# Values of the last batch's closing in seven products, gated products on GpSimd

## The chip, the cores and the metric

The kernel runs on one core of one Trainium2 chip. The core has five engines that run side by side, each through its own queue in order: TensorE (PE; its weight loads are shown apart as PEld), VectorE (DVE), ScalarE (ACT), GpSimd (POOL) and SyncE (SP, which issues most of the DMAs). Matrix products land in PSUM, of which the kernel uses eight banks of 512 f32 numbers per partition; everything else is in SBUF. The metric is the time of one execution on the device in microseconds, and the figure for a kernel is the median of several runs.

## The reference

Two layers follow each other. The first is attention in which a query sees only the keys of its own cluster, the second a gated feed-forward layer:

```python
mask = q_assign[:, :, :, None] == k_assign[:, :, None, :]
scores = np.where(mask, scale * q @ k.T, -1e9)
attn = softmax(scores) @ v                       # 4 batches, 8 heads, 768 x 64
x = attn.transpose(0, 2, 1, 3).reshape(3072, 512)
gate = 1.0 / (1.0 + np.exp(-(x @ w_gate)))       # 512 x 1536
val = x @ w_val                                  # 512 x 1536
out = (gate * val) @ w_out                       # 1536 x 512
```

Inputs and output are f32; the kernel multiplies in f16 and adds in f32.

## The kernel before

The program is written out step by step, in an order that is set by hand: a table of numbers (`SCHED`) gives each piece of preparation a step at which it is issued, and each engine runs its instructions in the order of issue. There are 384 attention steps, 96 per batch. A step is one score product (`sc`, L1026), its exponential on ACT (`es`, L1031) and, a few steps later, three products with the values (`av`, L1049). Between them the feed-forward layer of the batch before is fed in: groups of four matmuls for a gate (`g`, L531, tanh on ACT at L537) and for a value (`v`, L547), joined on DVE into `hT` (L552).

Scores, gates, values and logits (`lg`, L435) share a ring of four PSUM banks; two further pairs of banks are named `o` and `av`. A bank is taken again when the last operation that reads its old content is done.

The attention output is kept as x/2, so that the gate is tanh(x/2) + 1 = 2 sigmoid(x), and times (x/2) w_val that is gate times value.

The last batch has no attention behind it that could hide its feed-forward layer. It runs in `closing`. The hidden units come in 12 column blocks of 128, the 768 tokens in two halves of 384. Two column blocks (`FC0`) are done plainly, four matmuls for each block and half. The other ten form five column pairs, and the gates of a pair (two blocks by two halves) come as a 2 x 2 block product in seven products in place of eight (Strassen-Winograd). Each of the seven is two matmuls of 384 columns. They need four differences of the weights (`T` 1 to 4, made by `fin_weights`, one DVE operation for each, L602; eight in all for the two halves of `wg`) and four of the tokens (`S`, by `fin_tokens`, L616).

The class `Unit` holds a pair. Its products p1, p6, p7 and p4 add up in one PSUM bank `x`, and after each of them the bank's content is one step of the result: ACT copies it out (`c1`, `c12`, `c22`, and for p4 the last gate itself). p5 and p3 add up in a second bank `y`, p2 has a third; DVE adds these to the copies (`plus`, L650), and ACT takes the tanh. The values of a pair are computed in the plain way, one group of four matmuls for each block and half, in the period of the next pair (`Unit.v`, `hidden`). So a period of `closing` has 14 matmuls for the gates of one pair and 16 for the values of the pair before: 30.

What follows is the product with `w_out`, also in seven products, over three pairs of token blocks (`m0`, `ma`, `mb`); it needs sums of `hT` that DVE makes (`Sums.make`, called as `part`), and ends with the stores. The scratch tiles of `closing` are taken from the pool of the transposed heads, `T`; in the trace all of them bear that name.

Of the kernel before, what the change touches and what calls it, by code (L numbers as in the profile page):

```python
# [99 lines left out]
def kernel(  # L100
# [18 lines left out]
    NCH = S // 128  # L119
# [466 lines left out]
    def fin_weights(i, t):  # L586

        fin_room()
        a = FC0 // 2 if i == 0 else 0
        q = lambda k, j: wg[i][:, 2 * k : 2 * k + 2].rearrange(  # L590
            "p d (q j) f -> p d q j f", j=2
        )[:, :, a:, j]
        tw = lambda t: fin["kq"[i], (t - 1) // 2][:, (t - 1) % 2].rearrange(
            "p (d q f) -> p d q f", d=2, q=3
        )
        fin["T", i, t] = tw(t)
# [5 lines left out]
        DVE.tensor_tensor(cut(z), cut(x), cut(y), ALU.subtract)  # L602
# [25 lines left out]
    def fin_plain(xT, fc, blk):  # L628
        b, st = B - 1, []

        def gate():
            if fc == 0:
                need(*(("x", b, p, 3 * blk + c) for p in range(NP) for c in range(3)))
                HB[b, blk] = htp.tile([128, NFC, 384], HP, name="hT")
            g = fin_group(xT, 0, fc, blk)
            st.append(thp.tile([128, 384], FP, name="th"))
            ACT.activation(st[0], g, AF.Tanh)

        return [(NDC * 163, gate), (NDC * 163, lambda: hidden(xT, fc, blk, st[0]))]

    def hidden(xT, fc, blk, th):
        w = fin_group(xT, 1, fc, blk)
        DVE.scalar_tensor_tensor(HB[B - 1, blk][:, fc], th, 1.0, w, ALU.add, ALU.mult)  # L643

    def closing(xT):
# [5 lines left out]
        fin_tokens(xT, 4)  # L651
        room = [tp.tile([128, 12, 128], HP, tag="T", name="T") for _ in range(7)]
        slot = []
        for t in room[:4]:
# [4 lines left out]
        for m, n in ((m0, 0), (ma, 0), (mb, 1)):  # L659
            for i in (1, 2, 3):  # L660
                if n == 0:
                    m.of[i] = sump.tile([128, HF, 128], HP, tag="sum", name="sum")
                else:
                    m.of[i] = room[4 + i // 2][:, HF * (i % 2) : HF * (i % 2) + HF]
        m0.of[4], ma.of[4], mb.of[4] = room[4][:, 0:HF], room[6][:, 0:HF], room[6][:, HF:12]

        class Unit:
            def __init__(u, n, f):
                u.f, u.i, u.q = f, f // WQ, f % WQ // 2
                n = n % 2  # L670
                u.c1, u.c12, u.c22, u.c21 = slot[4 * n : 4 * n + 4]

            def mm(u, o, k, start, stop):
                T_ = lambda t, d: fin["T", u.i, t][:, d, u.q, :]
                W_ = lambda k_, j, d: wg[u.i][:, 2 * k_ + d, (u.f + j) % WQ, :]
# [13 lines left out]

            def p1(u):  # L690
                u.x = out_bank()[:, 0:384]
                u.mm(u.x, 1, True, True)
                ACT.activation(u.c1, u.x, AF.Copy)

            def p5(u):
                u.y = avp.tile([128, 512], FP, tag="av", name="av")[:, 0:384]
                u.mm(u.y, 5, True, True)

            def p6(u):
                u.mm(u.x, 6, False, True)  # L700
                ACT.activation(u.c12, u.x, AF.Copy)

            def p2(u):
                z = bank(512, name="gz")[:, 0:384]
                u.mm(z, 2, True, True)
                plus(u.c1, z, u.c1)

            def p7(u):
                u.mm(u.x, 7, False, True)
                ACT.activation(u.c22, u.x, AF.Copy)  # L710
                ACT.activation(u.c1, u.c1, AF.Tanh)

            def sum22(u):
                plus(u.c22, u.y, u.c22)

            def p4(u):
                u.mm(u.x, 4, False, True)
                ACT.activation(u.c21, u.x, AF.Tanh)
                ACT.activation(u.c22, u.c22, AF.Tanh)

            def p3(u):
                u.mm(u.y, 3, False, True)
                plus(u.c12, u.y, u.c12)

            def tanh12(u):
                ACT.activation(u.c12, u.c12, AF.Tanh)
# [5 lines left out]
        seq = []  # L732
        units = [Unit(n, f) for n, f in enumerate((6, 2, 8, 4, 10))]
        old = [f for fc in range(FC0) for _, f in fin_plain(xT, fc, 1)]
        def part(i, m, c0, c1, eng=None):
            return lambda: m.make(i, c0, c1, eng)

        extra = {
            3: [part(3, m0, 0, 4), part(3, ma, 0, 4)],
            4: [part(1, m0, 0, 4), part(2, m0, 0, 4)],  # L740
        }
        for n, u in enumerate(units):
            w = old if n == 0 else [lambda i=i, u=units[n - 1]: u.v(i) for i in range(4)]
            l = units[n - 1] if n else None
            ex = list(extra.get(n, []))
            e = lambda k: [ex.pop(0) for _ in range(min(k, len(ex)))]
            seq += [u.p1, w[0]] + ([l.p3] if l else []) + e(1) + [u.p5, u.p6]
            seq += ([l.tanh12] if l else []) + [w[1], u.p2, u.p7, w[2], u.sum22]
            seq += [w[3]] + e(1) + [u.p4]
# [54 lines left out]
        u = units[-1]  # L804
        both = lambda m, *c: [part(1, m, *c), part(2, m, *c)]
        seq += [lambda: u.v(0), part(1, ma, 0, 4), u.p3, u.tanh12, p0(1), lambda: u.v(1), part(2, ma, 0, 4), pa(1)]
        seq += [lambda: u.v(2), *both(m0, 4, HF), pb(1), lambda: u.v(3), l0([(0, HD)]), *both(ma, 4, HF)]
        seq += [la([(0, HD)]), part(1, mb, 0, HF), p0(6), part(2, mb, 0, HF), p0(5)]
        seq += [part(3, m0, 4, HF), part(3, ma, 4, HF), pa(6), part(4, m0, 0, HF), pa(5), part(3, mb, 0, HF)]
        seq += [p0(7), part(4, ma, 0, HF), pb(6), part(4, mb, 0, HF), pb(5)]  # L810
        seq += [pa(7), p0(4), p0(3), pb(7), pa(4), pa(3), pb(4), pb(3), lb([(0, HD // 2), (HD // 2, HD)])]
# [273 lines left out]
    def at(i, f):  # L1085
        bg.setdefault(max(i, step_no[0] - 0.5), []).append(f)
# [575 lines left out]
    for b in range(B):  # L1662
        xT = xtp.tile([128, NDC, S], HP, tag="xTb", name="xTb")
        key = min(b, 1)
        for i in range(2 if b else NPT):
            u = BASE[b] + (DONE0[i] if b == 0 else 96 - 12 * halved(b) if i == 0 else 96)
            lag = SCHED.get(f"lag{key}{i}", 8)
            if b == B - 1:
                if i == 0:
                    at(u + lag, lambda xT=xT: queue.extend(a for fc in range(FC0) for a in fin_plain(xT, fc, 0)))  # L1670
                    at(u + SCHED.get("fs1", 9), lambda xT=xT: (fin_tokens(xT, 1), fin_tokens(xT, 2)))
                    at(BASE[b] + 48 + SCHED.get("fs3", 17), lambda xT=xT: fin_tokens(xT, 3))
                    for k, s_ in enumerate(SCHED["fw"]):
                        at(s_, lambda k=k: fin_weights(1 - k // 4, 1 + k % 4))
# [56 lines left out]
```

## Time and profile before

| | |
|---|---|
| median of 3 runs | 321.93 us (321.38 to 322.49) |
| profiled execution | 320.28 us |
| its span, first to last instruction | 318.5 us |
| granted TensorE clock | 1.00 |
| attention steps, first score to last | about 9 to 269 us |
| `closing` with the plain column blocks | from 271.6 us |
| five pairs' periods | 274.2 to 299.3 us |
| output product | to 315.1 us (last matmul) |

The profile is one execution. Times in its rows are microseconds from the span's start. In a row of the timeline stand start, duration, engine, line, operation, and output from input, with the number of instructions that were merged, and in brackets the idle time of the engine before it with what ended it. A group of matmuls is drawn to the end of its last result, which overlaps the start of the next group. In a row of groups stand the busy time, the mean duration of one in ns, and the idle time before them.

### The profile page before, as it was taken

To read this page: it belongs to the slowest core of one execution; us is meant where nothing else is said; L and a number is where in the kernel's file an instruction comes from. 1 tells how busy PE (TensorE), PEld (TensorE's weight loads), DVE (VectorE), ACT (ScalarE), POOL (GpSimd) and SP (SyncE) were. 2 spreads that over 40 slices of the span, in tenths; PEclk is the share of its full clock that TensorE was granted. 3 is DMA by queue.
4 is the path that set the end of the run, shared out by engine and by line. 5 is a ranking of instruction groups with operands and counts; after the bars stand their busy time and mean duration, and the time that the engine had idled before them with its cause. 6 is when DMAs were issued, how large, how long until landed. Compare 5 with 4: busy or idle time off the path is not lost.

```text
span 318.5 us, 9195 instructions
## 1 busy us (share of the span) xinstructions
PE 312.2 (98%) x3500; PEld 221.1 (69%) x3500; DVE 233.7 (73%) x615; ACT 240.4 (75%) x545; POOL 109.0 (34%) x145
## 2 busy tenths in 40 slices
PE   7999999999999999999999999999999999999995
PEld 5888666766766666666777678666777678666685
DVE  6899656778687777686779678776766777668873
ACT  6688998797889887877767786887878886466521
POOL 5888454244434275423233342523202111000000
PEclk9999999999999999999999999999999999999999
DMA  7999998748859988977775555872612120300014
GB/s 197 374 266 187 262 158 132 180 95 244 243 102 178 188 231 133 204 211 149 110 204 139 180 111 147 255 106 52 112 24 67 42 27 20 138 3 0 1 35 165
DMA packets 77996, 45.16 MB, mean 142 GB/s; under 512 B 56896, under 2 KB 75520, under 8 KB 77952
## 3 DMA queue, kind: packets, MB, share of 16 engines
q1 hardware_dynamic: 73840, 39.66, 51.3%
q0 software_dynamic: 3680, 4.72, 8.9%
q8 instruction: 27, 0.44, 0.6%
q10 hardware_dynamic: 432, 0.20, 0.2%
q14 instruction: 17, 0.14, 0.2%
HBM read 28.34 MB, written 6.29 MB: 109 GB/s over the span
## 4 chain that ended last, share of the span: by engine, by line
PE 95%; DVE 2%; POOL 1%; issue 0%; ACT 0%; POOLq 0%; DVEq 0%
PE sc L1026 19%; PE g L531 15%; PE v L547 15%; PE av L1049 11%; PE o L954 9%; PE v L622 5%; PE o L825 5%; PE lg L435 2%; PE o L685 2%; PE o_end L763 2%; PE lg L422 1%; PE o L763 1%; PE av L763 1%; PE av L685 1%; PE t_ps L1275 1%; PE oh_ps L1335 1%
## 5 line engine op out<-in xcount | busy, mean ns | idle before, releaser
L1031 ACT ACTIVATE es<-sc 128x384 f16<-128x384 f32 x384 | 174.1, 492 | 38.6 <-PE sc L1026 29.9
L1026 PE MATMUL sc<-T 128*128 128x384 f16 x384 | 117.5, 326 | 0.4 <-DVE T L1356 0.4
L1049 PEld LDWEIGHTS <-es 128*128 128x128 f16 x1152 | 81.3, 98 | 35.1 <-ACT es L1031 0.2
L1049 PE MATMUL av<-va,es 128*128 128x65 f16 x1152 | 97.6, 194 | 0.0
L552 DVE SCALAR_TENSOR_TENSOR hT<-th,v 128x384 f16<-128x384 f32 x72 | 39.8, 553 | 38.3 <-PE av L1049 34.1
L531 PE MATMUL g<-xTb,wg 128*128 128x384 f16 x288 | 58.5, 326 | 0.2 <-DVE hT L552 0.2
L547 PE MATMUL v<-xTb,wv 128*128 128x384 f16 x288 | 58.6, 326 | 0.1
L376 POOL TENSOR_TENSOR xp<-t,rec 128x384 f16<-128x384 f32 (+1 forms) x30 | 21.6, 721 | 96.9 <-DVE rec L373 48.1
L537 ACT ACTIVATE th<-g 128x384 f32<-128x384 f32 x72 | 35.4, 491 | 8.7 <-PE g L531 6.7
L531 PEld LDWEIGHTS <-wg 128*128 128x128 f16 x288 | 27.9, 97 | 14.3 <-issue 0.4
L547 PEld LDWEIGHTS <-wv 128*128 128x128 f16 x288 | 28.0, 98 | 13.9 <-issue 0.3
L1026 PEld LDWEIGHTS <-T 128*128 128x128 f16 x384 | 37.1, 97 | 0.7 <-DVE T L1356 0.7
L1592 POOL TENSOR_TENSOR hl<-kraw,hl 128x384 f16<-128x384 f32 x22 | 20.2, 920 | 41.4 <-DVE hl L1591 24.3
L1592 POOL TENSOR_TENSOR hl<-qraw,hl 128x384 f16<-128x384 f32 x22 | 21.2, 962 | 11.1 <-DVE hl L1591 11.1
L825 PE MATMUL o<-wo,hT 128*128 128x512 f16 x72 | 19.9, 379 | 0.0
L371 DVE TENSOR_TENSOR t<-av,sv 128x390 f32<-128x390 f32 (+1 forms) x30 | 14.4, 480 | 7.2 <-PE av L1049 5.2
L622 PE MATMUL v<-xTb,wv 128*128 128x384 f16 x96 | 18.9, 326 | 0.0
L901 DVE TENSOR_TENSOR ob<-o,ob 128x256 f32<-128x256 f32 (+1 forms) x28 | 15.0, 549 | 4.7 <-PE o L954 3.2
L954 PE MATMUL o<-wo,hT 128*128 128x256 f16 x108 | 16.8, 273 | 0.0
L954 PEld LDWEIGHTS <-sum 128*128 128x128 f16 x144 | 14.0, 97 | 3.3
L643 DVE SCALAR_TENSOR_TENSOR hT<-T,v 128x384 f16<-128x384 f32 x20 | 11.0, 552 | 5.3 <-PE v L622 5.3
L450 DVE TENSOR_REDUCE lgs<-lg 128x192 f32<-128x384 f32 x23 | 12.7, 551 | 2.3 <-PE lg L435 2.3
(207 smaller groups left out, 445.2 us busy)
## 6 DMA issues: line engine op xcount, KB each, us to landing
vraw<-in_v_dram SPq DMA_DIRECT2D x15, 384.0 KB, 5.0
kraw<-in_k_dram SPq DMA_DIRECT2D x14, 384.0 KB, 4.9
qraw<-in_q_dram SPq DMA_DIRECT2D x12, 384.0 KB, 4.1
out_dram<-ob SPq DMA_DIRECT2D x17, 256.0 KB, 2.2
wg<-in_moe_w_gate_dram POOLq DMA_DIRECT2D x2, 768.0 KB, 9.6
wv<-in_moe_w_val_dram POOLq DMA_DIRECT2D x2, 768.0 KB, 10.5
wo<-in_moe_w_out_dram POOLq DMA_DIRECT2D x2, 768.0 KB, 9.4
T<-ohT SPq DMA_DIRECT2D x44, 24.0 KB, 1.9
```

Source lines behind the costliest of these rows:

```text
L376: (eng or POOL).tensor_tensor(x, t[:, 0:nq, 0:64], bcast(rec[:, 0:nq], 64), ALU.mult)
L531: PE.matmul(out=g[:, 0:n], lhsT=wg[fc // WQ][:, dc, fc % WQ, :], rhs=xT[:, dc, t0 : t0 + n], start=(dc == 0), stop=(dc == NDC - 1),)
L537: ACT.activation(th[:, 0:n], g[:, 0:n], AF.Tanh)
L547: PE.matmul(out=w[:, 0:n], lhsT=wv[fc // WQ][:, dc, fc % WQ, :], rhs=xT[:, dc, t0 : t0 + n], start=(dc == 0), stop=(dc == NDC - 1),)
L552: DVE.scalar_tensor_tensor(HB[b, blk][:, fc, 0:n], st[0][:, 0:n], 1.0, w[:, 0:n], ALU.add, ALU.mult)
L622: PE.matmul(out=o[:, 0:384], lhsT=w[:, dc, fc % WQ, :], rhs=xT[:, dc, 384 * blk : 384 * blk + 384], start=(dc == 0), stop=(dc == NDC - 1),)
L825: PE.matmul(out=o, lhsT=HB[b, blk][:, fc, bass.ts(t, 128)], rhs=wo[fc // WON][:, fc % WON, :], start=(fc == 0), stop=(fc == NFC - 1),)
L954: PE.matmul(out=st[z][:, e], lhsT=a[:, c, :], rhs=rhs[:, c, :], start=start and c + e == 0, stop=c == HF - 1, skip_group_check=True,)
L1026: PE.matmul(out=sc.rearrange("p (c t) -> p c t", t=128), lhsT=s["k"], rhs=s["q"], start=True, stop=True,)
L1031: ACT.activation(es, sc, AF.Exp, scale=SCALE)
L1049: PE.matmul(out=av[:, a0 + s["c0"] + i, :], lhsT=s["es"][:, bass.ts(i, 128)], rhs=VA[b, p][:, e, s["j"], :], start=(first and i == 0 and a ...
L1592: POOL.tensor_tensor(hl[:, :, 64:128], r, hl[:, :, 0:64], ALU.subtract)
```

## The change

The values of the first four pairs of `closing` are computed in seven products as well. The fifth pair keeps its four plain groups. What follows from it in the code:

- `fin_weights` makes four differences for each half of `wv` too, eight more DVE operations. Those of `wg` are issued at steps 327 to 344 in place of 354 to 371, and those of `wv` at the old steps. They are stored in the four `hl` tiles.
- `Unit` has a flag `w` (0 gate, 1 value). A value unit has its bank `x` from the `av` pair, `y` and the bank of p2 come from the ring. The values' p1 is taken out by DVE (`double`), the two other copies by ACT, with the factor 2 in them or in the sum (`twice`).
- The gate is now a sigmoid with scale 2, and the value carries the factor 2. This needs another function table on ACT; a small activation ahead of the first gate (`ACT.activation(r1, ones[:, 0:1], AF.Sigmoid)`) has it loaded.
- Three of the four gated products of a value unit (gate times value) go to POOL (`gated`); the fourth reads PSUM and stays on DVE (`out21`). The fifth pair's stay on DVE.
- A period is written anew: gate products of pair n, value products p1, p6, p5, p7, p2 of pair n-1, and its p4 and p3 in the period after. A full period has 28 matmuls.
- The pairs' order is 6, 2, 4, 8, 10 in place of 6, 2, 8, 4, 10. The sums for the output product are cut in other pieces, three of the sum tiles and the three fourth sums lie in the `vraw` tiles, and the order behind the last pair is rewritten.
- In the attention of the last batch one pick of clusters (the second head of the third head pair) is issued one step earlier.

```diff
-    ..., "fw": [354, 356, 357, 359, 364, 366, 370, 371], "END": 0,
+    ..., "fwg": [327, 327, 331, 331.5, 332, 341, 341, 344],
+    "fwv": [354, 356, 357, 359, 364, 366, 370, 371], "b3p2pk1": -28.5, "END": 0,
...
-            ACT.activation(st[0], g, AF.Tanh)
+            ACT.activation(st[0], g, AF.Sigmoid, scale=2.0)
...
-        DVE.scalar_tensor_tensor(HB[B - 1, blk][:, fc], th, 1.0, w, ALU.add, ALU.mult)
+        DVE.scalar_tensor_tensor(HB[B - 1, blk][:, fc], w, 2.0, th, ALU.mult, ALU.mult)
...
+        twice = lambda dst, a, z: DVE.scalar_tensor_tensor(dst, a, 2.0, z, ALU.mult, ALU.add)
+        ACT.activation(r1, ones[:, 0:1], AF.Sigmoid)
...
+            def copy(u, dst):
+                ACT.activation(dst, u.x, AF.Copy, scale=2.0 if u.w else 1.0)
+
+            def gated(u, j, blk, z, th):
+                POOL.tensor_tensor(HB[b, blk][:, u.f + j], z, th, ALU.mult)
+
             def p1(u):
-                u.x = out_bank()[:, 0:384]
+                u.x = (avp.tile([128, 512], FP, tag="av", name="av") if u.w else out_bank())[:, 0:384]
                 u.mm(u.x, 1, True, True)
-                ACT.activation(u.c1, u.x, AF.Copy)
+                if not u.w:
+                    u.copy(u.c1)
+
+            def double(u):
+                DVE.tensor_scalar(u.c1, u.x, 2.0, None, ALU.mult)
...
             def p2(u):
-                z = bank(512, name="gz")[:, 0:384]
+                z = bank(512, name="z")[:, 0:384]
                 u.mm(z, 2, True, True)
-                plus(u.c1, z, u.c1)
+                (twice if u.w else plus)(u.c1, z, u.c1)
+                if u.w:
+                    u.gated(0, 1, u.c1, u.g.c1)
...
             def p4(u):
                 u.mm(u.x, 4, False, True)
-                ACT.activation(u.c21, u.x, AF.Tanh)
-                ACT.activation(u.c22, u.c22, AF.Tanh)
+                if not u.w:
+                    ACT.activation(u.c21, u.x, AF.Sigmoid, scale=2.0)
+
+            def out21(u):
+                DVE.scalar_tensor_tensor(HB[b, 0][:, u.f], u.x, 2.0, u.g.c21, ALU.mult, ALU.mult)
...
-            seq += [u.p1, w[0]] + ([l.p3] if l else []) + e(1) + [u.p5, u.p6]
-            seq += ([l.tanh12] if l else []) + [w[1], u.p2, u.p7, w[2], u.sum22]
-            seq += [w[3]] + e(1) + [u.p4]
+        extra = {3: [part(1, m0, 0, 2)], 4: [part(2, m0, 0, 2), part(3, m0)]}
+        for n in range(1, len(G)):
+            g, v, l = G[n], V[n - 1], G[n - 1]
+            o = V[n - 2] if n > 1 else None
+            old = lambda *f: [getattr(o, x) for x in f] if o else []
+            seq += [
+                g.p1, lambda l=l: l.gate(l.c22), *old("p4"), v.p1, v.double, l.p3,
+                g.p6, lambda l=l: l.gate(l.c12), *old("p3"), g.p2, *old("out21"), v.p6,
+                g.p7, lambda g=g: g.gate(g.c1), g.p5, g.sum22, *extra.get(n, []), v.p5, v.p7,
+                g.p4, v.sum22, v.p2,
+            ]
...
+        u = G[-1]
+        seq += [
+            p0(1), lambda: u.gate(u.c22), V[-1].p4, u.p3, lambda: u.gate(u.c12), V[-1].p3, V[-1].out21, lambda: u.v(0), lambda: u.v(1), pa(1),
+            lambda: u.v(2), part(1, m0, 2), part(2, m0, 2), pb(1), lambda: u.v(3), l0([(0, HD)]),
+            part(1, ma), part(2, ma), la([(0, HD)]), part(1, mb), p0(6), part(2, mb), p0(5),
...
```

How it moves instructions shows at three places. The first is ACT's queue in the third pair's period of `closing`, before and now. `o_` is the pair's gate bank, `av_` the bank of the values of the pair before, `T_` scratch.

```order
L693 ACTIVATE T_6229<-o_6343 128x384
L701 ACTIVATE T_6229<-o_6343 128x384
L726 ACTIVATE T_6231<-T_6231 128x384
L710 ACTIVATE T_6230<-o_6343 128x384
L711 ACTIVATE T_6229<-T_6229 128x384
L718 ACTIVATE T_6230<-o_6343 128x384
L719 ACTIVATE T_6230<-T_6230 128x384
```
```order
L705 ACTIVATE T_6221<-o_6355 128x384
L758 ACTIVATE T_6218<-T_6218 128x384
L705 ACTIVATE T_6221<-o_6355 128x384
L758 ACTIVATE T_6220<-T_6220 128x384
L705 ACTIVATE T_6216<-av_6362 128x384
L705 ACTIVATE T_6217<-o_6355 128x384
L758 ACTIVATE T_6221<-T_6221 128x384
L705 ACTIVATE T_6216<-av_6362 128x384
L746 ACTIVATE T_6217<-o_6355 128x384
```

Seven operations became nine: the two copies from `av_` are new, and the sigmoid of the older c12 (`T_6220`) now stands ahead of the first of them.

The second is DVE's queue in the same period, now: the values' doubling, the gate's older c12, the older values' c12, the gate's c1, the older values' product from PSUM, the gate's c22, and the values' c22 and c1.

```order
L717 TENSOR_SCALAR T_6215<-av_6362 128x384
L656 TENSOR_TENSOR T_6220<-y_6335,T_6220 128x384
L657 SCALAR_TENSOR_TENSOR T_6214<-y_6339,T_6214 128x384
L656 TENSOR_TENSOR T_6221<-z_6377,T_6221 128x384
L749 SCALAR_TENSOR_TENSOR hT_6231<-av_6362,T_6218 128x384
L656 TENSOR_TENSOR T_6217<-y_6389,T_6217 128x384
L657 SCALAR_TENSOR_TENSOR T_6216<-y_6393,T_6216 128x384
L657 SCALAR_TENSOR_TENSOR T_6215<-z_6404,T_6215 128x384
```

Before, DVE had seven in a period: three sums and four products of gate and value.

The third is DVE in the attention of the last batch, at the pick that is issued earlier (the reduce of the logits `lgs`, its maximum and the comparison `oh1`), before and now:

```order
L1591 CAST hl_5035<-qraw_4794 128x6x64
L552 SCALAR_TENSOR_TENSOR hT_4772<-th_5086,v_5108 128x384
L450 TENSOR_REDUCE lgs_5121<-lg_5091 128x192
L461 TENSOR_REDUCE mx_5123<-lgs_5121 128x12
L463 TENSOR_TENSOR oh1_135<-lgs_5121,mx_5123 128x6x16 x2
L470 TENSOR_SCALAR oh1_135<-oh1_135 128x6x16
L1591 CAST hl_5145<-kraw_4786 128x6x64
```
```order
L1631 CAST hl_5035<-qraw_4794 128x6x64
L451 TENSOR_REDUCE lgs_5108<-lg_5091 128x192
L462 TENSOR_REDUCE mx_5110<-lgs_5108 128x12
L464 TENSOR_TENSOR oh1_135<-lgs_5108,mx_5110 128x6x16 x2
L471 TENSOR_SCALAR oh1_135<-oh1_135 128x6x16
L553 SCALAR_TENSOR_TENSOR hT_4772<-th_5086,v_5115 128x384
L1631 CAST hl_5145<-kraw_4786 128x6x64
```

The pick moved ahead of one `hT`, and with it the bank of the logits is given back earlier; the scores two groups on take that bank, and the gate group behind them one that an exponential has read.

More of the change, by code (lines that the diff above doesn't have):

```diff
@@ L584, in fin_room, with fin_weights @@
                     )
-    def fin_weights(i, t):
+    def fin_weights(w, i, t):
         fin_room()
+        if w == 1 and ("h", 0) not in fin:
+            for n in range(4):
+                fin["h", n] = hlp.tile([128, 12, 128], HP, tag="hl", name="hl").rearrange(
+                    "p c x -> p (c x)"
+                ).rearrange("p (h x) -> p h x", h=2)
         a = FC0 // 2 if i == 0 else 0
-        q = lambda k, j: wg[i][:, 2 * k : 2 * k + 2].rearrange(
+        q = lambda k, j: (wg, wv)[w][i][:, 2 * k : 2 * k + 2].rearrange(
             "p d (q j) f -> p d q j f", j=2
         )[:, :, a:, j]
[L593 to L596, printed above, removed]
+        tw = lambda t: (fin["h", 2 * i + (t - 1) // 2] if w else fin["kq"[i], (t - 1) // 2])[
+            :, (t - 1) % 2
+        ].rearrange("p (d q f) -> p d q f", d=2, q=3)
+        fin["T", w, i, t] = tw(t)
         z, x, y = {
@@ L730, in v, with part @@
                 hidden(xT, u.f + j, blk, th)
[L732 to L746, printed above, removed]
-            seq += [u.p1, w[0]] + ([l.p3] if l else []) + e(1) + [u.p5, u.p6]
-            seq += ([l.tanh12] if l else []) + [w[1], u.p2, u.p7, w[2], u.sum22]
-            seq += [w[3]] + e(1) + [u.p4]
+        def part(i, m, c0=0, c1=HF):
+            return lambda: m.make(i, c0, c1)
+        FS = (6, 2, 4, 8, 10)
+        G = [Unit(0, n, f) for n, f in enumerate(FS)]
+        V = [Unit(1, n, f) for n, f in enumerate(FS[:-1])]
+        for g, v in zip(G, V):
+            v.g = g
+        u = G[0]
+        w = [f for fc in range(FC0) for _, f in fin_plain(xT, fc, 1)]
+        seq += [
+            u.p1, w[0], lambda u=u: u.p5(avp.tile([128, 512], FP, tag="av", name="av")), u.p6, w[1],
+            u.p2, u.p7, lambda u=u: u.gate(u.c1), w[2], u.sum22, w[3], u.p4,
+        ]
[9 more added lines that the diff above has]
+                g.p4, v.sum22, v.p2,
+            ]
         def pair(m, bk):
```

76 lines of the change are left out of this document (41 added, 35 removed), and 2 rows, old and new, of the table SCHED.

## The prediction

> **What bounds the kernel now.** I read the page first, then its chain of waits, then a table of windows over the end of the span, then the timelines of PE, ACT and DVE there.
>
> ```profile
> PE 312.2 (98%) x3500; PEld 221.1 (69%) x3500; DVE 233.7 (73%) x615; ACT 240.4 (75%) x545; POOL 109.0 (34%) x145
> PE 95%; DVE 2%; POOL 1%; issue 0%; ACT 0%; POOLq 0%; DVEq 0%
> ```
>
> The first row is the page's busy time, the second the chain that ended last: 95% of it is TensorE. The windows of 4 us in the closing say the same of the stage that is edited:
>
> ```profile
> core 0: us, PE busy (x) PEld busy (x) DVE busy (x) ACT busy (x) POOL busy (x), PEclk, DMA share, GB/s
> 284.00:288.00 4.00, 4.00 (x26) 2.43 (x25) 2.65 (x6) 2.93 (x7) 0.00 (x0) 1.00 0.02 6
> 288.00:292.00 4.00, 4.00 (x27) 2.40 (x25) 3.19 (x8) 2.31 (x7) 0.00 (x0) 1.00 0.00 0
> ```
>
> PE has no gap, at a granted clock of 1.00; DVE, ACT and POOL have room. A busy PE need not be PE at its pace, so here is one period of the closing, with PE's waiting places:
>
> ```profile
> 275.86 0.81 PE L622 MATMUL v<-xTb,wv 128*128 128x384 f16 x4
> 276.83 0.49 PE L685 MATMUL o<-qraw 128*128 128x384 f16 x2
> ...
> 283.66 0.49 PE L685 MATMUL o<-xTb,wg 128*128 128x384 f16 x2
> 283.98 0.81 PE L622 MATMUL v<-xTb,wv 128*128 128x384 f16 x4
> 284.63 0.49 PE L685 MATMUL av<-qraw,wg 128*128 128x384 f16 x2
> ...
> 288.53 0.49 PE L685 MATMUL o<-xTb,wg 128*128 128x384 f16 x2
> ```
>
> From 283.66 to 288.53 are 4.87 us, in which the program has 14 matmuls of the gate's seven products and 16 of the values: 30, or 0.1625 us each. Four of them take 284.63 - 283.98 = 0.65, the same. PE runs here at one pace, without a wait, so a matmul taken away is 0.1625 us off the end as long as no wait takes its place.
>
> **The products removed.** Four of the five column pairs (those at 6, 2, 4, 8) get their values in 14 matmuls instead of 16. That is 8 matmuls: 8 x 0.1625 = **-1.30 us**. The Trainium skill (TensorE: Matmul & The Clock Gate, Back-to-back issue gap) gives about 131 ns for a matmul of 512 columns in a sustained stream, and N/2.4 + 2.5 ns for an isolated one; by the first the eight would be worth at most 8 x 0.131 = 1.05 us, by the second 1.30. The trace agrees with the second (0.1625 us at 384 columns).
>
> **The new period.** A full period (third to fifth pair) is now 28 matmuls, 4.55 us: fourteen products 0.325 apart. The hazard is that the seven products of a pair add up in one PSUM bank and are copied out between: the next product must wait until the copy has read the bank. The durations, with ACT's and DVE's rows:
>
> ```profile
> 277.36 0.49 ACT L710 ACTIVATE T<-o 128x384 f32<-128x384 f32 x1 [0.81 <-PE o L685]
> ...
> 278.98 0.49 ACT L718 ACTIVATE T<-o 128x384 f32<-128x384 f32 x1 [0.25 <-PE o L685]
> 279.37 0.51 ACT L719 ACTIVATE T<-T 128x384 f32<-128x384 f32 x1
> 279.78 0.48 ACT L693 ACTIVATE T<-o 128x384 f32<-128x384 f32 x1
> ```
> ```profile
> 276.78 0.55 DVE L643 SCALAR_TENSOR_TENSOR hT<-th,v 128x384 f16<-128x384 f32 x1 [1.25 <-PE v L622]
> 277.25 0.55 DVE L650 TENSOR_TENSOR T<-gz,T 128x384 f32<-128x384 f32 x1
> ```
>
> A product ends 0.49 after its start; ACT begins 0.04 later (276.83 + 0.49 to 277.36) and is done after 0.49; it takes an operation every 0.39 to 0.41. DVE begins 0.11 after PE's end (275.86 + 0.81 to 276.78) and takes one every 0.47. PE resumes 0.06 after what it waited for (the pair of rows further down: 216.86 + 0.55 to 217.47; that is DVE to PE, and I take it for ACT to PE too). So from a product to the next one on its bank 0.49 + 0.04 + 0.49 + 0.06 = 1.08 us must pass. In a full period the pairs p1 and p6, p6 and p7, p7 and p4 are four products apart, for gates and values alike: 1.30, a spare of 0.22. (The values' p1 goes to DVE: 0.49 + 0.11 + 0.55 + 0.06 = 1.21, and p6 comes 1.625 later.) The tightest is the gate's p7: its copy stands on ACT behind the copy of the values' p6, which begins 2.275 + 0.49 + 0.04 = 2.81 into the period; so it begins at 3.21, ends at 3.70 and frees the bank at 3.76, and p4 is due at 3.90: spare 0.14. ACT has nine operations, 9 x 0.40 = 3.6 of 4.55 us; DVE eight, 8 x 0.47 = 3.76. So 0 in the full periods. From both sides: below nothing is impossible, as PE has no gap to close; above, a hand-over 0.30 later than the rows say costs 0.16 at the tightest place, and with the others some 0.3 in each of three periods, +0.9. I take 0, since the spares come from rows of this very stage.
>
> **The second pair's period is short.** It has no older values to finish: p1, values' p1, the older p3, p6 stand three apart, 0.975, less than 1.08. ACT moreover still has the sigmoid of the first pair's p4 (ending 0.165 into the period) ahead of the copy: sigmoid at 0.21, copy at 0.61 to 1.10, bank free at 1.16, a stall of 0.19. Then p6 ends at 1.65, its copy runs 1.69 to 2.18, free at 2.24, p7 due at 1.16 + 0.975 = 2.14: 0.10. Together **+0.29 us**, between 0 (if p6 is let in earlier than the copy's end) and 0.5.
>
> **ACT's table.** The sigmoid needs a table that the exponentials don't have:
>
> ```profile
> 1.65 1.28 ACT L287 ACT_TABLE_LOAD   x1 [1.65 <-PEq L1715]
> 2.94 0.20 ACT L287 ACTIVATE r<-wo 128x1 f32<-128x1 f16 x1
> ...
> 268.74 1.07 ACT L1031 ACTIVATE es<-sc 128x384 f16<-128x384 f32 x2 [0.42 <-PE sc L1026]
> 272.48 0.49 ACT L637 ACTIVATE th<-g 128x384 f32<-128x384 f32 x1 [2.67 <-PE g L622]
> ```
>
> The load and its dummy take 1.28 + 0.20 in a gap of 2.67 us between the last exponential and the first gate: 0, with 1.2 to spare; without that cover, +1.5 on the first gate.
>
> **POOL's products.** Twelve multiplications of 128x384 f32 go to an engine that was idle in the closing. The rows nearest to them:
>
> ```profile
> L1592 POOL TENSOR_TENSOR hl<-qraw,hl 128x384 f16<-128x384 f32 x22 | 21.2, 962 | 11.1 <-DVE hl L1591 11.1
> L376 POOL TENSOR_TENSOR xp<-t,rec 128x384 f16<-128x384 f32 x18 | 15.5, 859 | 73.4 <-DVE rec L373 32.9 <-DMA T<-ohT 23.1 <-issue 14.9
> ```
>
> Three in a period are 3 x 0.96 = 2.9 of 4.55 us; the last (values of the pair at 8) has some 3 us until the sums of the output product read it. 0; at twice the price POOL would fall behind by 1.2 us a period, and its last would come about when it is read. The Trainium skill (GPSIMD Engine Reference, Engine selection and Specifications) speaks against this: elementwise work is about twice as slow there as on VectorE, and the two share SBUF interfaces, contended by VectorE operations with two SBUF inputs. By it the sum stays: on DVE the three would make 11 x 0.47 = 5.2 us, more than the period, and the period's DVE operations have one input in PSUM, but for the sums. That two such operands don't collide no row here shows.
>
> **The attention part: eight more weight differences on DVE.** The gate's move to where DVE ran at 230 to 244, the values' take their old places. The price is from the two groups of 250 us, the cover from DVE's idle time before the rows that follow:
>
> ```profile
> L602 DVE TENSOR_TENSOR qraw<-wg x2: 551/552/553, 250.5 to 252.6; 128x768 f16<-128x768 f16 x2
> L602 DVE TENSOR_TENSOR kraw<-wg x2: 396/442/489, 256.4 to 260.4; 128x512 f16<-128x512 f16 x2
> ```
> ```profile
> 231.44 0.55 DVE L552 SCALAR_TENSOR_TENSOR hT<-th,v 128x384 f16<-128x384 f32 x1 [1.47 <-PE av L1049]
> ...
> 234.71 0.56 DVE L552 SCALAR_TENSOR_TENSOR hT<-th,v 128x384 f16<-128x384 f32 x1 [1.91 <-PE av L1049]
> ...
> 241.00 0.55 DVE L552 SCALAR_TENSOR_TENSOR hT<-th,v 128x384 f16<-128x384 f32 x1 [1.27 <-PE av L1049]
> ...
> 243.97 0.56 DVE L552 SCALAR_TENSOR_TENSOR hT<-th,v 128x384 f16<-128x384 f32 x1 [0.75 <-PE av L1049]
> ```
>
> Four of 0.55 go, two by two, into the idle 1.47 and 1.91; one of 0.44 stands ahead of the pick after 234.71; three come between 241.00 and 243.97, 3 x 0.35 to 0.44 against 0.75 idle, so that the hT there is 0.3 to 0.5 late. What is late next is the PSUM bank of its values; it is wanted again several groups later. 0, and up to +0.4 if that cover is gone. The values' own eight cost what the gate's cost there before: 0.
>
> **One pick earlier.** At 217.47 PE shows one of its rare gaps:
>
> ```profile
> 215.48 0.45 PE L435 MATMUL lg<-cm,T 128*128 128x32 f16 x12
> ...
> 217.47 0.81 PE L531 MATMUL g<-xTb,wg 128*128 128x384 f16 x4 [0.20 <-DVE hT L552]
> ```
> ```profile
> 216.86 0.55 DVE L552 SCALAR_TENSOR_TENSOR hT<-th,v 128x384 f16<-128x384 f32 x1 [1.54 <-PE av L1049]
> 217.33 0.55 DVE L450 TENSOR_REDUCE lgs<-lg 128x192 f32<-128x384 f32 x1
> ...
> 218.86 0.35 DVE L1591 CAST hl<-kraw 128x384 f16<-128x384 f32 x1
> ```
>
> The logits hold a bank of the ring until the reduce reads them, and the gate group g must take the bank that hT frees at 217.41. With the pick ahead of hT the reduce can run from 215.93 + 0.11 = 216.04 to 216.59, in DVE's idle 1.54; the scores at 216.94 take the logits' bank, and g one that an exponential freed. The pick lasts 218.86 - 217.33 = 1.53, so hT comes at 217.57, 0.71 later, and ends at 218.13; its bank is next taken by the scores that stood at 219.10. **-0.20 us**; 0 if hT's lateness stalls another group.
>
> **The sum.** -1.30 + 0.29 - 0.20 = -1.21. The profiled execution took 320.28 (its span 318.5 and 1.78 around it), so 319.07 in its terms. It lies 1.65 under the median of the runs shown, 321.93, from which I count the forecast: 321.93 - 1.21 = **320.7 us**.
>
> **Rivals.** *A, the copies are late everywhere.* All of the new order hangs on spares of 0.14 to 0.22, where the old one had more: p1 and p6 stood 1.625 apart. With 0.3 lost in each of three periods and the attention's 0.4 not hidden: 320.7 + 0.9 + 0.4 = 322.0, no change. Against it stand the even spacings above.
>
> *B, ACT's queue stands behind a gate that waits for DVE: slower.* In each period the sigmoid of the older c12 is ahead of the copies of the values' p6 and the gate's p7, and waits for DVE's sum, which follows the values' doubling. The doubling can start at 0.65 + 0.49 + 0.11 = 1.25, the sum at 1.72, ending at 2.27; the sigmoid at 2.31 lets ACT go at 2.72, 0.09 before the copy of p6 at 2.81. With p4's spare that is 0.23, and from there each us that DVE is late is one that PE stands: 0.94 late (two DVE operations) costs 0.71 in each of four periods, 2.8, so **323.5**; it decides against the change from a lateness of 0.53 on, where 4 x 0.30 uses up the gain. For it: DVE's last two sums of a period wait for its last products, the last begins at 3.575 + 0.49 + 0.04 + 0.49 + 0.03 + 0.47 = 5.1, or 0.55 into the next period, and in the fourth and fifth period sums for the output of 0.2 to 0.7 are put ahead. Against: DVE is free again at 1.02, and the doubling can't start before 1.25, so 0.2 is absorbed.
>
> *C, the saved matmuls were hidden anyway.* PEld is busy only 2.4 of 4.0 us in the windows; if PE's full row covered a pace that something else sets, eight fewer would change nothing, 321.9. The equal 0.1625 in the period and in a group of four speaks against it. The Trainium skill (Perfetto Trace Analysis, Identifying the Most-Contended Engine) holds matmul busy time to be a poor measure and asks for the weight loads' share; by that rule PE has 40% of room here, which the trace bears out for the weight loads but not for the matmuls' pace.
>
> **Chances.** Forecast 0.55, A 0.20, B 0.17, C 0.08. The forecast's own range is 320.2 to 321.2 (stall 0 to 0.5, runs that differ by 0.3 from their median). The range runs from 319.9 (no stall, and 0.5 of scatter: the runs shown lie 321.38 to 322.49) to 322.8, past A and C; what is left out is most of B. A measurement of this kernel can tell 0.3%, 0.97 us, from no change, and the forecast clears that by 0.24 only: faster gets 0.48 of the 0.55 and 0.06 of A in half its measure, in all 0.54; slower gets B and 0.02 of A, 0.19; same the rest, 0.27.
>
> **What would show it.** Right: PE without a gap from the third pair on, p1 of one pair to that of the next 4.55 us apart; gaps of 0.19 and 0.10 ahead of the second pair's p6 and p7, released by ACT; no gap at the g near 217. Wrong: gaps that come again in each period ahead of the gate's p4 (A) or of the values' p7 with ACT waiting for DVE (B); POOL's products above 1.5 us; new gaps at 232 to 246.

## The result, and the profile after

| | before | after |
|---|---|---|
| median of 16 runs each, side by side | 320.52 us (319.96 to 322.65) | 319.09 us (318.38 to 320.46) |
| profiled execution | 320.28 us | 319.12 us |
| its span | 318.5 us | 317.3 us |
| logits near 217 (`lg`) to the first `g` of the closing | 215.48 to 271.63: 56.15 us | 215.77 to 271.56: 55.79 us |
| first `g` of the closing to the start of the last twelve matmuls | 271.63 to 314.31: 42.68 us | 271.56 to 313.17: 41.61 us |

By the medians the change is 1.43 us faster. The ratio over all the runs is 0.9946 (95% interval 0.9927 to 0.9965), which is 1.7 us, between 1.1 and 2.3: before has more long runs among its sixteen, and they weigh more there than in the median. The two stages of the table give 0.36 + 1.07 = 1.43, from one execution of each kernel; the spans differ by 1.2 only, since their starts differ too (the `lg` stands 0.29 later in the second). The three runs of before that the prediction had were all among the long ones: the sixteen fall into ten between 319.96 and 320.94 and six between 321.38 and 322.65, and those three are of the six.

The busy times and the chain of waits on the page of the changed kernel:

```profile
PE 310.0 (98%) x3492; PEld 218.8 (69%) x3492; DVE 238.6 (75%) x623; ACT 244.9 (77%) x555; POOL 120.9 (38%) x157
PE 93%; DMA 2%; DVE 1%; POOL 1%; SPq 1%; issue 0%; ACT 0%; DVEq 0%
```

Eight matmuls fewer, and TensorE is still what the end hangs on. The windows over the same stretch of the closing as before (columns as there):

```profile
284.00:288.00 4.00, 4.00 (x26) 2.43 (x25) 3.56 (x8) 3.38 (x9) 2.51 (x3) 1.00 0.02 4
288.00:292.00 4.00, 4.00 (x27) 2.40 (x25) 3.66 (x9) 3.58 (x9) 2.97 (x3) 1.00 0.01 2
```

PE has no gap, but DVE and ACT, at 2.65 and 2.93 in the first of these windows before, now stand at 3.56 and 3.38 of 4.00. Most of the room that the old period had is used up. PE's timeline from the second pair's period on:

```profile
278.71 0.49 PE L699 MATMUL o<-xTb,wg 128*128 128x384 f16 x2
279.03 0.49 PE L699 MATMUL av<-xTb,wv 128*128 128x384 f16 x2
279.36 0.49 PE L699 MATMUL av<-qraw,wg 128*128 128x384 f16 x2
279.83 0.48 PE L699 MATMUL o<-kraw 128*128 128x384 f16 x2
280.16 0.49 PE L699 MATMUL z<-xTb,wg 128*128 128x384 f16 x2
280.48 0.49 PE L699 MATMUL av<-kraw,hl 128*128 128x384 f16 x2
280.90 0.48 PE L699 MATMUL o<-qraw,kraw 128*128 128x384 f16 x2
...
282.84 0.49 PE L699 MATMUL o<-xTb,wg 128*128 128x384 f16 x2
...
287.39 0.49 PE L699 MATMUL o<-xTb,wg 128*128 128x384 f16 x2
...
291.94 0.49 PE L699 MATMUL o<-xTb,wg 128*128 128x384 f16 x2
```

Products start 0.325 apart, except ahead of p6 (279.36 to 279.83) and p7 (280.48 to 280.90): 0.145 and 0.095 too much. From the third pair on, p1 (`o<-xTb,wg`) comes at 282.84, 287.39 and 291.94: 4.55 apart, as forecast. No idle time is drawn for the two stalls, because the drawn end of a product overlaps the next one's start by 0.16; they show only in the starts. What PE waited for is in ACT's timeline, the copies of the gate's bank after p1 and after p6:

```profile
279.30 0.48 ACT L705 ACTIVATE T<-o 128x384 f32<-128x384 f32 x1
...
280.35 0.49 ACT L705 ACTIVATE T<-o 128x384 f32<-128x384 f32 x1 [0.16 <-PE o L699]
```

They end at 279.78 and 280.84, and p6 and p7 start 0.05 and 0.06 later.

The other places that the prediction named, in the timelines of ACT, POOL and PE:

```profile
269.76 1.28 ACT L658 ACT_TABLE_LOAD   x1
271.06 0.20 ACT L658 ACTIVATE r<-ones 128x1 f32<-128x1 f16 x1
272.41 0.49 ACT L643 ACTIVATE th<-g 128x384 f32<-128x384 f32 x1 [1.15 <-PE g L628]
```
```profile
L708 POOL TENSOR_TENSOR hT<-T 128x384 f16<-128x384 f32 x12 | 11.8, 1001 | 16.2 <-DVE T L657 15.6 <-ACT T L758 0.6
```
```profile
217.23 0.33 PE L1066 MATMUL sc<-T 128*128 128x384 f16 x1
217.39 0.81 PE L532 MATMUL g<-xTb,wg 128*128 128x384 f16 x4
```

The table load is hidden with 1.15 us to spare. POOL's products take 1.00 each (priced 0.96). The gap ahead of `g` near 217 is gone.

### The profile page after: what moved, and what is told of

Its sections match the earlier page's. It is cut to its first block, busy times and chain, and to the rows that moved or that the text cites. A ratio compares the mean times of both kernels' runs of the same rounds, so it can differ in the third digit from the quotient of the medians.

```text
span 317.3 us, 9228 instructions
## 1 busy us (share of the span) xinstructions
PE 310.0 (98%) x3492; PEld 218.8 (69%) x3492; DVE 238.6 (75%) x623; ACT 244.9 (77%) x555; POOL 120.9 (38%) x157
## 2 busy tenths in 40 slices
DMA packets 77996, 45.16 MB, mean 142 GB/s; under 512 B 56896, under 2 KB 75520, under 8 KB 77952
## 4 chain that ended last, share of the span: by engine, by line
PE 93%; DMA 2%; DVE 1%; POOL 1%; SPq 1%; issue 0%; ACT 0%; DVEq 0%
PE sc L1066 19%; PE g L532 15%; PE v L548 15%; PE av L1089 11%; PE o L994 9%; PE o L865 5%; PE lg L436 2%; PE o L699 2%; PE o_end L802 2%; PE av L699 2%; DMA kraw<-in_k_dram 2%; PE v L628 2%; PE y L699 2%; PE o L802 1%; PE av L802 1%; PE z L699 1%
## 5 line engine op out<-in xcount | busy, mean ns | idle before, releaser
L548 PE MATMUL v<-xTb,wv 128*128 128x384 f16 x288 | 58.5, 326 | 0.1
L708 POOL TENSOR_TENSOR hT<-T 128x384 f16<-128x384 f32 x12 | 11.8, 1001 | 16.2 <-DVE T L657 15.6
L324 POOL CAST va<-vraw 128x768 f16<-128x768 f32 x15 | 13.1, 873 | 2.4 <-DMA vraw<-in_v_dram 2.4
```

Of the source, the lines that this page charges most:

```text
L548: PE.matmul(out=w[:, 0:n], lhsT=wv[fc // WQ][:, dc, fc % WQ, :], rhs=xT[:, dc, t0 : t0 + n], start=(dc == 0), stop=(dc == NDC - 1),)
```

## The experiments

"Closing" is the time from its first `g` to the start of the last twelve matmuls: 42.68 before, 41.61 with the change. It is free of what differs between executions ahead of it.

### The change again

No edit.

> The changed kernel once more, so that the next kernels have it beside them on one chip. Theory (the edit is worth 1.30 us of products, 0.24 us given back in two gaps of the second pair's period, and 0.37 us from the pick): 1.4 us under the kernel before, ratio 0.9955. Rival (0.20 us from the pick, as the gap in the row said): 1.25 us under it, 0.9961.

Median 319.1 of 7 runs, ratio 0.9958 (0.9933 to 0.9982), closing 41.61, the part from `lg` to the closing 55.79: both stages as before to 0.01. The span is 316.7 in place of 317.3, and `lg` stands 0.61 earlier (215.16): all of that difference is in the first 215 us.

### The pick: taken out of the change, and put alone into the kernel before

```diff
-    "fwv": [354, ..., 371], "b3p2pk1": -28.5, "END": 0,
+    "fwv": [354, ..., 371], "END": 0,
```

> The changed kernel with the pick at its old step. Theory: the gate group near 217 us waits for DVE's hT again, and the group's start moves by 0.37 us against the logits ahead of it (the row will show 0.20 of it as idle); 0.37 us slower than the changed kernel. Rival (the pick is worth what the row shows): 0.20 us. Rival 2 (hT's lateness costs elsewhere what the pick gains): no difference.

Median 319.5 (11 runs), ratio 0.9965 (0.9953 to 0.9977). The gap is back, by the timeline of PE:

```profile
216.91 0.33 PE L1066 MATMUL sc<-T 128*128 128x384 f16 x1
217.44 0.81 PE L532 MATMUL g<-xTb,wg 128*128 128x384 f16 x4 [0.20 <-DVE hT L553]
```

The stretch from `lg` to the closing is 56.16, against 55.79: the pick is worth 0.37, not the 0.20 in the bracket. The score product takes 0.16 to the next start where nothing waits (217.23 to 217.39 in the changed kernel), here 0.53. That 56.16 equals before's 56.15 also says that the eight further weight differences in the attention cost nothing. The closing is 41.70, with one gap of 0.10 ahead of a p4 that no other execution of this closing shows. ACT's copy of p7 starts 0.86 after p7 there, against 0.59 in the changed kernel; what held ACT is not visible.

The same entry, `"b3p2pk1": -28.5`, in the kernel before:

> The kernel before with nothing but the pick moved. Theory: the gap near 217 us goes, 0.37 us faster than before, closing unchanged (first gate group to last matmul 43.5 us). Rival: 0.20 us, or 0 if another group stalls for the late hT.

Median 320.04 (12 runs), ratio 0.9988 (0.9972 to 1.0004): too small for the timing. The stages tell it: 55.79 ahead of the closing, 42.67 in it. So 0.36 of the change's 1.43 is the pick, and it has nothing to do with the products.

### The second pair's period filled

The first pair's period has four plain groups of matmuls among its products. The last of them moves into the second pair's short period, between p6 and p7; there p2 goes ahead of p6, and p1 goes forward, ahead of the first pair's p4:

```diff
-            u.p2, u.p7, lambda u=u: u.gate(u.c1), w[2], u.sum22, w[3], u.p4,
+            u.p2, u.p7, lambda u=u: u.gate(u.c1), w[2], u.sum22, G[1].p1, u.p4,
...
+            if n == 1:
+                seq += [
+                    lambda l=l: l.gate(l.c22), v.p1, v.double, l.p3, g.p2,
+                    g.p6, lambda l=l: l.gate(l.c12), w[3], v.p6,
+                    g.p7, lambda g=g: g.gate(g.c1), g.p5, g.sum22, v.p5, v.p7,
+                    g.p4, v.sum22, v.p2,
+                ]
+                continue
```

> The changed kernel with the second pair's period rewritten: its first product is issued ahead of the first pair's last one, its p2 ahead of p6, and one plain value group of the first pair's period stands between p6 and p7, so that no two products on one bank are less than four apart. Theory (the two gaps come from three products' distance): both gaps go, 0.24 us less in closing, 0.24 us faster than the changed kernel. Rival (the gaps come from ACT being behind there): they move to other products of that period and nothing is gained.

Median 318.87 (9 runs), ratio 0.9951 (0.9929 to 0.9972), closing 41.38: both stalls are gone, 0.23 better than the change.

> Again the order without the second pair's two stalls, for a tighter time. Closing 41.38 as before (41.61 in the change); a median 0.1 to 0.3 under the change's 319.1, so 318.8 to 319.0, ratio to the kernel before 0.994 to 0.995. Rival: the stalls only move, 319.1.

Median 318.68 (12 runs), ratio 0.9948 (0.993 to 0.9966), closing 41.37. The gain of 0.23 is shown by the stage, twice; the medians (0.2 and 0.4 under the change's) lean the same way, though their intervals overlap with it. It is the best of the kernels here.

### Eight matmuls put back

The values' p2 is issued twice into the same bank:

```diff
                 u.mm(z, 2, True, True)
+                if u.w:
+                    u.mm(z, 2, True, True)
```

> The changed kernel with the two matmuls of each value unit's p2 issued twice, eight matmuls of 384 columns more, everything else alike. Theory (PE's pace bounds the closing): first gate group to the start of the last twelve matmuls 41.61 + 8 x 0.1625 = 42.91 us. Rival (PE's row covers a pace that something else sets): less, down to 41.6.

320.36 in one run; closing 42.91, no wait of PE in it. 42.91 - 41.61 = 1.30: eight times 0.1625, to the hundredth. Rival C, by which the matmuls were hidden anyway, is out.

### The gated products on DVE

```diff
-                POOL.tensor_tensor(HB[b, blk][:, u.f + j], z, th, ALU.mult)
+                DVE.tensor_tensor(HB[b, blk][:, u.f + j], z, th, ALU.mult)
```

> The changed kernel with its twelve gated products on DVE in place of POOL. Theory: DVE has 11 x 0.47 = 5.2 us in a period of 4.55, so DVE bounds three periods, and PE waits for it: closing 2 to 4 us longer than 41.61. Rival (a product costs half on DVE of what it costs on POOL, so it is better kept there): no longer, or shorter.

Median 323.28 (4 runs), ratio 1.0091 (1.0074 to 1.0108), closing 45.86: 4.25 worse, a little over the 2 to 4 expected, and worse than before. On DVE a product takes about half of what it takes on POOL, by the groups of DVE between 270 and 300 us (nine of the twelve products):

```profile
L708 DVE TENSOR_TENSOR hT<-T 128x384 f16<-128x384 f32 x9 | 5.0, 558 | 0.3
```

But DVE had eight operations a period and now has eleven; p1 comes 5.23, 5.64 and 5.71 us apart (282.65, 287.88, 293.52, then 299.23 for what follows), where 4.55 is PE's own. Eleven times 0.47 are 5.2 us, and the two longer periods have the sums for the output product besides. So in this order the edit is a loss without POOL: the slower engine is the better one here, because it was idle.

### DVE made late: one operation, two operations

An addition of 128x384 f32 behind each values' doubling, which nobody reads (two of them in the second kernel):

```diff
                 DVE.tensor_scalar(u.c1, u.x, 2.0, None, ALU.mult)
+                for _ in range(1):
+                    t = thp.tile([128, 384], FP, name="th")
+                    DVE.tensor_tensor(t, u.c1, u.c1, ALU.add)
```

> The changed kernel with one more DVE operation of 128x384 f32 behind the values' doubling in each of the four periods (it writes a scratch tile that nothing reads). Theory (ACT's queue stands behind the sigmoid that waits for DVE's sum): the spare in the profile is 0.17 on ACT and 0.16 ahead of p4, so 0.5 us of lateness costs about 0.2 us a period, closing 0.5 to 1.0 us longer than 41.61. Rival (DVE has room, nine times 0.47 are 4.2 of 4.55 us): 0.

> The same with two more DVE operations. Theory: 1.0 us of lateness costs about 0.65 us a period, closing 2.0 to 3.0 us longer than 41.61, back at the kernel before or over it. Rival (only DVE's sum of busy time counts, ten times 0.47 are 4.7 of 4.55 us): 0.15 a period, 0.5 us.

322.55 and 324.31 in one run each, closing 45.16 and 47.05: 3.5 and 5.4 worse than the change, far over both expectations. The timelines of DVE and of POOL in the first of them show why:

```profile
289.93 0.56 DVE L717 TENSOR_SCALAR T<-av 128x384 f32<-128x384 f32 x1
290.52 1.29 DVE L720 TENSOR_TENSOR th<-T 128x384 f32<-128x384 f32 x1
291.73 0.55 DVE L656 TENSOR_TENSOR T<-y,T 128x384 f32<-128x384 f32 x1
```
```profile
289.44 1.96 POOL L708 TENSOR_TENSOR hT<-T 128x384 f16<-128x384 f32 x2 [1.16 <-DVE T L657]
```

The addition takes 1.29 where 0.55 was reckoned, and ends 0.41 after POOL's two products (289.44 + 1.96 = 291.40). It does so in each of the last three periods, and in the second pair's, where POOL has nothing to do yet, it takes the usual time (the four of them average 1.13: three of 1.37, 1.29 and 1.30, and one of 0.56). With two additions the pair took 1.76 to 1.84. So the experiment had made DVE 1.33 and 1.81 late, not 0.47 and 0.94. What that does is rival B's mechanism as the prediction has it, in ACT's timeline of the same kernel:

```profile
290.56 0.49 ACT L705 ACTIVATE T<-o 128x384 f32<-128x384 f32 x1 [0.40 <-PE o L699]
292.31 0.52 ACT L761 ACTIVATE T<-T 128x384 f32<-128x384 f32 x1 [1.26 <-DVE T L656]
292.74 0.47 ACT L705 ACTIVATE T<-av 128x384 f32<-128x384 f32 x1
```

The sigmoid (L761) waits 1.26 us for DVE's sum, and the copies that PE needs stand behind it.

### DVE late by an operation that reads PSUM

```diff
+                t = thp.tile([128, 384], FP, name="th")
+                DVE.tensor_tensor(t, u.x, u.c1, ALU.add)
```

> Leaves nothing out; as dve_one_late, but the extra DVE addition behind each values' doubling has one operand in PSUM in place of two in SBUF. Theory (the extra op of dve_one_late took 1.30 us where it overlapped POOL's products and 0.56 where it did not, because two SBUF operands have to wait until POOL's multiplication is done; the price per period is lateness minus about 0.25): the op takes 0.56 in all four places, DVE is 0.47 late, and the loss is 0.2 to 0.35 in each of four periods: closing 42.4 to 43.0 from the first g to the last twelve matmuls (41.61 in the change), a median of 319.9 to 320.5. Rival (DVE is simply full, the kind of operand is no matter): the op takes 1.3 again, closing 45.2, some 322.6.

Median 320.25 (10 runs), ratio 0.9988 (0.9971 to 1.0004), closing 42.86: 1.25 worse than the change, as expected. The addition takes 0.56 everywhere, beside POOL's products too:

```profile
290.88 0.56 DVE L717 TENSOR_SCALAR T<-av 128x384 f32<-128x384 f32 x1
291.47 0.56 DVE L719 TENSOR_TENSOR th<-av,T 128x384 f32<-128x384 f32 x1
291.94 0.55 DVE L656 TENSOR_TENSOR T<-y,T 128x384 f32<-128x384 f32 x1
```
```profile
290.39 1.96 POOL L708 TENSOR_TENSOR hT<-T 128x384 f16<-128x384 f32 x2 [1.16 <-DVE T L657]
```

With this kernel the price of lateness has three points. Lateness is the time from the doubling to the sum that follows it, less the 0.47 of the changed kernel; the period is the fourth pair's, from p1 to p1 (289.63 to 294.51, 288.68 to 294.29, 289.51 to 295.60), and what is lost is counted over 4.55:

| | doubling to sum | late by | period | lost | late less lost |
|---|---|---|---|---|---|
| one addition from PSUM | 290.88 to 291.94 | 0.59 | 4.88 | 0.33 | 0.26 |
| one addition from SBUF | 289.93 to 291.73 | 1.33 | 5.61 | 1.06 | 0.27 |
| two additions from SBUF | 290.76 to 293.04 | 1.81 | 6.09 | 1.54 | 0.27 |

In the third pair's period the same three differences are 0.35, 0.34 and 0.35: there the doubling stands 0.07 to 0.08 nearer to p1.

### Which operands meet POOL

One extra operation a period, of another kind in each:

```diff
+                t = thp.tile([128, 384], FP, name="th")
+                if u.f == FS[1]:
+                    DVE.tensor_scalar(t, u.c1, 2.0, None, ALU.mult)
+                elif u.f == FS[2]:
+                    t = t.bitcast(HP).rearrange("p (d x) -> p d x", d=2)
+                    DVE.tensor_tensor(t, fin["S", 1], fin["S", 2], ALU.add)
+                else:
+                    DVE.tensor_tensor(t, u.x, u.c1, ALU.add)
```

> Leaves nothing out; one extra DVE operation behind the values' doubling, of another kind in each period: PSUM and SBUF f32 (second pair's period, POOL idle), one SBUF input f32 (third), two SBUF inputs f16 of 128x768 (fourth), PSUM and SBUF f32 (fifth, POOL busy). Theory: both with PSUM take 0.56; the one with two f16 inputs ends some 0.4 to 0.5 after POOL's second product, so takes 1.2 to 1.4 against 0.55 alone; the one with a single SBUF input is open: 0.3 to 0.56 if one input never meets POOL, 1.1 or more if it does. Rival: every operation beside POOL's is stretched alike.

320.55 in one run, closing 43.35. DVE's and POOL's timelines, third and fourth period:

```profile
284.62 1.16 DVE L720 TENSOR_SCALAR th<-T 128x384 f32<-128x384 f32 x1
...
289.98 0.55 DVE L723 TENSOR_TENSOR th<-kraw 128x768 f16<-128x768 f16 x1
```
```profile
283.61 1.95 POOL L708 TENSOR_TENSOR hT<-T 128x384 f16<-128x384 f32 x2 [11.58 <-DVE T L657]
...
289.03 2.37 POOL L708 TENSOR_TENSOR hT<-T 128x384 f16<-128x384 f32 x2 [1.17 <-DVE T L657]
```

A single f32 input from SBUF seems to wait too: the operation ends 0.22 after POOL's pair (285.78 against 285.56); how long it takes beside an idle POOL is in no run here. The fourth period came out the other way than expected: the f16 addition took its usual 0.55, and POOL's pair took 2.37 in place of 1.96. It started 0.95 after the pair did, just between the two products (0.96 apart), and there DVE was first and POOL waited. Both with a PSUM operand took 0.56. So in these places, where DVE reads only SBUF, the two take turns in whole operations, and whoever is first holds up the other. The Trainium skill (SBUF — State Buffer, Who interferes with whom) has this as a rule: the two engines share one pair of SBUF ports, held for a whole instruction, and a VectorE operation with two SBUF inputs or in a mode that uses both ports needs it. The two additions agree with it; whether the operation with one input ran in such a mode, no trace shows.

### POOL's products twice

```diff
                 POOL.tensor_tensor(HB[b, blk][:, u.f + j], z, th, ALU.mult)
+                POOL.tensor_tensor(HB[b, blk][:, u.f + j], z, th, ALU.mult)
```

> Leaves nothing out; each of POOL's twelve products is issued twice, so three in a period take 5.8 to 6.0 of 4.55 us. By the prediction's step POOL falls behind by 1.2 us a period and its last product comes about when the sums of the output product read it: 0 to 1.0 over the change (319.1 to 320.1). Rival: POOL's lateness reaches PE by the sums of hT on DVE (two SBUF inputs, they would wait for POOL's product in progress), 1 to 4 us: up to 323.

325.98 in one run, closing 49.39: 7.8 worse, more than either expected. At this price POOL is not only late at the end. ACT's and PE's timelines:

```profile
288.82 0.49 ACT L705 ACTIVATE T<-o 128x384 f32<-128x384 f32 x1 [0.87 <-POOL hT L709]
...
295.07 0.49 ACT L705 ACTIVATE T<-o 128x384 f32<-128x384 f32 x1 [1.14 <-POOL hT L709]
```
```profile
308.19 0.50 PE L803 MATMUL o_end<-wo,hT 128*128 128x256 f16 x3 [2.12 <-POOL hT L709]
```

A gate's copy goes into a scratch tile that an earlier product of POOL still has to read, so ACT waits for POOL, and PE for ACT; the fourth and fifth periods grow to 5.59 and 6.24 us (286.46, 292.05, 298.29), 2.7 of the 7.8. The rest is lost behind them, 2.12 of it where the output product waits for POOL's last one. POOL's own timeline has no idle time between its first product and its last (282.62 to 308.13). A sum of two `hT` that meets POOL takes 1.35 instead of 0.55.

## Why the prediction was wrong in its time, and right in its steps

**The step that failed** is the last one: "It lies 1.65 under the median of the runs shown, 321.93, from which I count the forecast: 321.93 - 1.21 = 320.7 us", and with it the range, whose lower end was counted from the same figure. The sum was made against the profiled execution, 320.28, and in its terms it gave 319.07; the median measured is 319.09. That these two lie so close is in part luck, as two errors cancel: the profiled execution lies a little under the median of before, and the gain was counted 0.22 too small. Sixteen runs of before have their median at 320.52, 0.24 from the profiled execution and 1.41 from the figure counted from. Three runs that all lay above the one execution whose rows carry the sum were a reason to reach down with the range to that execution's level, not to count from theirs.

**The removed matmuls, -1.30**: right; putting eight back costs 1.30.

**The full periods, 0**: right; 4.55 apart, no gap. The spare behind it, priced at 0.23 from hand-overs read off rows, measures 0.26 to 0.27 in the fourth period and 0.34 to 0.35 in the third.

**The second pair's stalls, +0.29**: right in place and cause, a little large: 0.145 + 0.095 = 0.24, and filling the period gains 0.23. The first was the one mis-sized (0.19): the copy ended 1.07 after p1 where 1.10 was reckoned, and p6 followed 0.05 later.

**The pick, -0.20**: right in its mechanism, too small. The bracket counts from the drawn end of the product before; start to start the stall was 0.37 (0.53 against 0.16). The three terms as measured, -1.30 + 0.24 - 0.37, give -1.43, the sum of the two stages; -1.21 was forecast. That the medians differ by the same 1.43 to the hundredth is luck, since the runs fix the gain only to between 1.1 and 2.3 us.

**The table load, 0**: right, and 1.15 to spare. **The attention's weight differences, 0**: right; the `hT` that was to be 0.3 to 0.5 late was 0.17 late (at 244.07 it is 27.49 ahead of the closing's first `g`; before, at 243.97, it was 27.66), and the stretch takes the same time with and without them.

**POOL's products, 0**: right at 1.00 us each. Their bound was wrong: "at twice the price POOL would fall behind by 1.2 us a period, and its last would come about when it is read" saw only the last reader, and put the lateness too low even for that one: the last product ended 37.50 after the closing's first `g`, against 28.78 in the changed kernel, 8.7 later, where some 3 were to spare. Doubled, they cost 7.8, through the scratch tiles and the last reader both.

**Two SBUF operands**: the prediction left open whether DVE and POOL collide. They do. The change escapes it because the DVE operations in its pairs' periods have one operand in PSUM, and its sums of `hT` at 291.57, 296.13 and 296.32 happen to lie in POOL's pauses (from 291.28 and from 295.82 on).

**Rival A**, late copies everywhere: no gap showed. **Rival B** did not happen, but its formula, lateness less 0.23 in each period, is what the three late kernels obey, with 0.26 to 0.35 in place of 0.23. **Rival C** is excluded by the eight matmuls put back.

## What to carry to other kernels

A term that rests on one execution's rows belongs to that execution's own time; where the runs shown lie elsewhere, the range has to hold both levels. Measure a stall from start to start against an undisturbed neighbour, since the idle time drawn can hide 0.16 of it, or all. When elementwise work is moved to GpSimd beside a busy VectorE, look at which VectorE operations have no operand in PSUM and at who next writes the tiles that GpSimd reads: with GpSimd busy for 2.96 of a period of 4.55 us the move was free, and with twice that it cost 7.8 us.

## What the runs showed of the hardware that was not expected

- A DVE operation that waits for POOL's is drawn as busy, not idle: 1.29 to 1.37 us for an addition that takes 0.56 in the same kernel while POOL is idle. A group with a mean between two values is where to look.
- A DVE operation that reads what the one just ahead of it wrote starts 0.59 after it, where others follow at 0.47 (in the late kernel with the PSUM operand 291.47 after 290.88, then 291.94 after 291.47; the f16 addition, which reads something else, 289.98 after 289.51).
- Three of the fourteen profiled executions have a wait of PE for a transfer at 120 to 122 us, in the attention, that the others lack. In PE's timeline of the late kernel with the PSUM operand:

```profile
122.37 0.47 PE L436 MATMUL lg<-cm,T 128*128 128x32 f16 x12 [1.37 <-DMA T<-hl]
```

  That execution took 322.01, against a median of 320.25. In the other two (both of the filled second pair) it is 1.2 and 1.3 us, at 319.35 and 320.44 against medians of 318.87 and 318.68. In the three of them the `lg` near 217 stands at 216.26 to 217.41, in the others at 214.83 to 215.77. The wait is somewhat smaller than the 1.8 us between the means of the longer six and the other ten runs of before; whether those six had it is not shown, since none of them was profiled.
